# Retention and a gated feed-forward network on one core: k by tokens moves into a fifth slot beside v, loaded with it in one transfer, and the order of the work is planned anew

## The chip, the cores and the metric

The kernel runs on one core of one Trainium2 chip. The metric is the device time in microseconds (us), the median of several runs. TensorE is called PE in the profile, its weight loads PEld, VectorE DVE, ScalarE ACT, GpSimd POOL, and the queue that issues the transfers SP.

## The reference

The inputs are q, k, v of shape (4, 8, 768, 64), w_in (512, 1024), conv_w (3, 1024), w_out (1024, 512), all float32.

```python
for t in range(S):                       # retention, per batch and head
    state = gamma * state + k[t] (x) v[t]
    y[t] = scale * q[t] @ state
x = y, heads side by side                # (4, 768, 512)
h = relu(x @ w_in)                       # (4, 768, 1024)
conv_out[t] = sum over k of conv_w[k] * h[t + k - 1]
out = (h * sigmoid(conv_out)) @ w_out    # (4, 768, 512)
```

## The kernel before

**Attention.** The 3,072 tokens are cut into 24 chunks of 128, each into two halves of 64. For chunk n, `load_qk(n)` brings q and k with the head dimension on partitions (512 KB), and `load_kv(n)` brings k and v with tokens on partitions. Before the change these are two transfers of 256 KB with rows of 2 KB: k into a tile `kn` of its own, which has two buffers, and v into slot 2 of the chunk's tile `rw`, which has three. Slot 3 of `rw` takes the carried state. `scale_v` multiplies v by decay factors, `masked` masks the scores. `mix(n, s)` is one visit of PE to half s of chunk n: matmuls for the state (`ps_st`), for y (`ps_y`) and for the next chunk's scores (`ps_s`), 64 of 64x64 in a usual visit, each with a weight load. `carry` (ACT) copies the state for the next visit, `decay` (DVE) makes x, `x_head` (ACT) and `x_rest` (DVE or POOL) split it into two parts in tile `xu`.

**Feed-forward.** Two chunks make a unit u of 256 tokens, 12 in all. `mm1(u, f)` is 12 matmuls of 128x258 (L643) for one of 8 slices of the hidden width; `relu`, `conv_tap`, `conv_side`, `gate`, `gated`, `g_head`, `g_rest` follow on ACT and DVE. `mm2(u, t, p)` is 6 matmuls of 128x512 (L699) for output tile t and pair p of hidden slices. There are 96 of `mm1` and 96 of `mm2`. The weights arrive as 64-bit numbers in 16 slices of 512 KB (buffer `g`, shared with the gate's output) and are turned into two float32 parts by a chain on ACT and DVE. For the first `SUMMED` slices PE does the last sum (`w_sum`, L609 to L611).

**Order.** Nothing is scheduled at run time: each engine, and SP's queue, works through its list in order. A planner, `plan`, plays the program with given durations, buffer counts (`BUFS`), a load rate (`BYTE`), and limits and lead times (`ATT_RATE`, `CONV_RATE`, `WINDOW`, `SLACK` and others), and the tasks are written out in the order of the start times that it finds. Where it finds PE waiting early on, it puts in filler matmuls on a zero tile (`keep_warm`, L388, 128x512), which PE works through like any others. In `plan`, `load_kv(n)` takes a `kn` buffer that `mix(n-2, 1)` gives back, and `load_qk(n)` an `rw` buffer that `mix(n-3, 1)` gives back.

Of the kernel before, what the change touches and what calls it, by code (L numbers as in the profile page):

```python
# [16 lines left out]
B, H, S, D = 4, 8, 768, 64  # L17
DM, DFF = H * D, 1024
P = 128
C = 64  # L20
NC = S // P
NPAIR = H // 2
# [16 lines left out]

BUFS = {
    "rw": 3, "kn": 2, "x": 2, "xu": 3, "g": 6, "m": 3, "es": 1, "h": 30, "cv": 2, "ps_s": 1, "ps_y": 2, "ps_m": 2, "ps_o": 2,
}


PE, DVE, ACT, POOL, DMA = "PE", "DVE", "ACT", "Pool", "DMA"
BYTE = 1 / 360

LATENCY, SAME = {DMA: 2600, PE: 250}, {DMA: 0, PE: 50}  # L50
OTHER = 60
# [8 lines left out]
MIX = 950  # L60
USE = {"scores": 0.25, "mix": 0.5, "mm1": 0.98, "mm2": 0.98, "w_sum": 0.98}

ATT_FIRST, ATT_RATE = 25, 6.5

CONV_FIRST, CONV_RATE, CONV_LAG = 0, 12.5, 27
SUM_LEAD, SUM_LEAD_OUT = 70, 238
AHEAD = 5517
WINDOW = {PE: 21000, POOL: 44250, DMA: 47450}
STAY = 48
PACE = 1.6  # L70

SLACK = {
    "x_rest": 21500, "halo": 22000, "w_in": 54000, "w_out": 28000, "mix": 55000, "carry": 57000,
    "masked": 54000, "make_gy": -7000, "x_head": 39000, "scores": 57500, "g_rest": 52500, "scale_v": 19500,
    "conv_w": 59000,
}

VECTOR_V, VECTOR_X, SUMMED = 36, 10, 5


PORT = {"scale_v", "x_rest", "w_clamp", "w_shift", "w_sign", "w_power", "w_low", "w_rest", "w_add", "conv_side", "gated",
# [2 lines left out]
def has_state(n, s):  # L84
    return (n % NC, s) != (NC - 1, 1)


def list_tasks():
# [3 lines left out]
    def task(key, engine, ns, after=(), take=None, free=None):  # L92
        tasks[key] = (engine, ns, [a for a in after if a], take, free)

    for n in range(N_CHUNKS):
        b, c = divmod(n, NC)
        u = n // NT
        task(("load_qk", n), DMA, 4 * P * D * H * 2 * BYTE, [n and ("load_qk", n - 1)], take="rw")
        after = [n and ("load_kv", n - 1), ("load_qk", n)]
        task(("load_kv", n), DMA, 4 * P * D * H * 2 * BYTE, after, take="kn")  # L100
        vector = n < VECTOR_V
        task(("scale_v", n), DVE if vector else POOL, 690 if vector else 1230, [("load_kv", n)])
        if n == 0:
            for s in range(2):
                task(("scores", 0, s), PE, 485, [("load_qk", 0), s and ("scores", 0, 0)], take=None if s else "ps_s")
        task(("masked", n), DVE, 690, [("mix", n - 1, 1) if n else ("scores", 0, 1)], free="ps_s")
        for s in range(2):

            prev = (n, 0) if s else (n - 1, 1) if c else (n - 1, 0) if b else None
            after = [("scale_v", n), ("masked", n), prev and ("carry", *prev)]  # L110
            after += [("mix", n, 0) if s else n and ("mix", n - 1, 1)]
            after += [n + 1 < N_CHUNKS and ("load_qk", n + 1)]
            take = None if s else "ps_y" if n + 1 == N_CHUNKS else ("ps_y", "ps_s")
            free = ("rw", "kn") if s and c < NC - 1 else "rw" if s else "kn" if c == NC - 1 else None
            task(("mix", n, s), PE, MIX, after, take, free)
            if has_state(n, s):
                task(("carry", n, s), ACT, 370, [("mix", n, s)])
        if n == 0:
            task(("load_gy",), DMA, 4 * P * NPAIR * P * BYTE)
        elif n < NC:  # L120
            task(("make_gy", c), ACT, 1300, [("load_gy",)])
        task(("decay", n), DVE, 690, [("mix", n, 1), ("make_gy", c) if c else ("load_gy",)], "x", "ps_y")
        if n % NT == 0:
            task(("x_tiles", u), POOL, 60, [u and ("x_tiles", u - 1)], take="xu")
        task(("x_head", n), ACT, 620, [("decay", n), ("x_tiles", u)])
        vector = n < VECTOR_X
        task(("x_rest", n), DVE if vector else POOL, 690 if vector else 1280, [("x_head", n)], free="x")
        if n % NT == NT - 1 and u % NU + 1 < NU:
            task(("halo", n, 1), POOL, 620, [("x_rest", n), ("x_tiles", u + 1)])
        if n % NT == 0 and u % NU > 0:  # L130
            task(("halo", n, -1), POOL, 620, [("x_rest", n), ("x_tiles", u - 1)])
# [3 lines left out]
    for i in range(CONV + 1):  # L135
        big = i < CONV
        ns = lambda t: t if big else 90
        if big:
            task(("load_w", i), DMA, 8 * P * DM * BYTE, [i and ("load_w", i - 1)], take="g")
        else:  # L140
# [20 lines left out]
    for u in range(N_UNITS):  # L161
        x = [("x_tiles", u)] + [("x_rest", NT * u + t) for t in range(NT)]
        x += [u % NU and ("halo", NT * u - 1, 1), u % NU + 1 < NU and ("halo", NT * u + NT, -1)]
        for f in range(NF):
# [3 lines left out]
                take="ps_m", free="xu" if f == NF - 1 else None,  # L168
            )
            p, odd = divmod(f, 2)  # L170
# [3 lines left out]
                take=None if odd else "cv",  # L174
# [14 lines left out]
        for t in range(NT):  # L189
            halves = 2 if (u, t) == LAST else 1  # L190
            for h in range(halves):
                for p in range(NF // 2):
# [5 lines left out]
                        take=None if p else "ps_o", free="g" if t == NT - 1 and h == halves - 1 else None,  # L198
# [41 lines left out]
def plan(tasks):  # L240
# [15 lines left out]
    for i, k in enumerate(tensor_sequence(tasks)):  # L256
        place[k], late[k] = i, t
        t += tasks[k][1] * PACE
    for k in reversed(topo):
# [4 lines left out]
    free = dict(FIRST)  # L264
    slots = {name: [0.0] * n for name, n in BUFS.items()}
    ready = {engine: {} for engine in free}
# [8 lines left out]
    def earliest(k, engine, t):  # L275
        for name in several(tasks[k][3]):
            if not slots[name]:
                return None
            t = max(t, min(slots[name]))
        if k[0] in PORT:  # L280
            t = max(t, port)
        return max(t, free[engine] + (SWITCH if engine == PE and last != KIND[k[0]] else 0))
# [4 lines left out]
    while len(start) < len(tasks):  # L287
        best = None
        for engine, some in ready.items():
            found = []  # L290
            for k, t in some.items():
                if engine != PE or place[k] < head + AHEAD:
                    t = earliest(k, engine, t)
                    if t is not None:
                        rank = place[k] - STAY * (KIND[k[0]] == last) if engine == PE else late[k]
                        found.append((t, rank, k))
            if found:
                limit = min(found)[0] + WINDOW.get(engine, 0)
                t, _, k = min((x for x in found if x[0] <= limit), key=lambda x: x[1])
# [39 lines left out]
def retention_then_gated_ffn(  # L339
# [13 lines left out]
    nc = tc.nc  # L353
# [12 lines left out]
    gvf_sb = const.tile([P, NC, 3, NPAIR], F32, name="gvf_sb")  # L366
# [7 lines left out]
    def buf(name, shape, dtype=F32):  # L374
        return pool.tile(shape, dtype, name=name, bufs=BUFS[name])

    def ps_buf(name, shape=(P, 512)):
        return psum.tile(list(shape), F32, name=name, bufs=BUFS[name])

# [8 lines left out]
            nc.tensor.matmul(ps, warm, warm.unsqueeze(1).broadcast_to([P, 4, P]), start=True, stop=True)  # L388


    rw, kns, s_ps, st_ps, y_ps, xt, xs = {}, {}, {}, {}, {}, {}, {}

    flat = lambda a: a.rearrange("p a s g c -> p a (s g c)")

    @emits
    def load_qk(n):

        rw[n] = buf("rw", [P, 4, 2, NPAIR, C])
        if n == 0:
            nc.gpsimd.dma_start(gvf_sb, gvf)  # L400
            nc.gpsimd.dma_start(mask_sb, mask)
        nc.sync.dma_start(flat(rw[n][:, :2]), qk[n])

    @emits
    def load_kv(n):

        kns[n] = buf("kn", [P, 2, NPAIR, C])
        nc.sync.dma_start(kns[n].rearrange("p s g c -> p (s g c)"), kv[n][:, 0])
        nc.sync.dma_start(flat(rw[n][:, 2:3]), kv[n][:, 1:])

    @emits
    def load_gy():
# [8 lines left out]
    @emits  # L421
    def scale_v(n):
        (nc.vector if n < VECTOR_V else nc.gpsimd).tensor_tensor(  # L423
            out=rw[n][:, 2], in0=rw[n][:, 2], in1=gvf_sb[:, n % NC, :2].unsqueeze(3).broadcast_to([P, 2, NPAIR, C]),
            op=ALU.mult,
        )

# [10 lines left out]
    def of_state(n, s):  # L438
        b, c = divmod(n, NC)
        first = (c, s) == (0, 0)  # L440
        if first:
            st_ps[b] = psum.tile([P, NPAIR, D], F32, name="ps_st")
        for g, j in heads:
            r = HALF[j]
            yield st_ps[b][r, g], kns[n][r, s, g], rw[n][r, 2, s, g], first and g == 0, c == NC - 1

    def of_y(n, s):
        if s == 0:
            y_ps[n] = ps_buf("ps_y", (P, NPAIR, 2, C))

        alone = n % NC == 0 and s == 0
        for g in range(NPAIR):
            for part, (w, x) in enumerate([(2, 1)] if alone else [(2, 1), (3, 0)]):
                for j in range(2):
                    y, r = y_ps[n][HALF[1 - j], g, s], HALF[j]
                    yield y, rw[n][r, w, s, g], rw[n][r, x, s, g], part == 0, part == 1 or alone
# [27 lines left out]
    @emits  # L484
    def carry(n, s):

        nc.scalar.copy(rw[n + s][:, 3, 1 - s], st_ps[n // NC])  # L487

    @emits
    def decay(n):  # L490
# [213 lines left out]
    def put(u, t, h):  # L704
# [5 lines left out]
        nc.sync.dma_start(out[r0 : r0 + P, cs], o[:, :n])  # L710

    start, more = plan(list_tasks())
    keep_warm(WARM_UP)
    for k in sorted(start, key=start.get):
# [55 lines left out]
```

## Time and profile before

| what | value |
|---|---|
| runs | 373.07, 375.35, 375.55 us; median 375.35 us |
| the profiled execution | 375.01 us, span 373.2 us |
| granted clock | 1.00 |
| PE busy | 361.2 us, 97% of the span |
| DVE, ACT, POOL busy | 259.3, 201.2, 31.8 us |
| read from HBM, written | 33.98 MB, 6.29 MB |

The span runs from the first to the last instruction of the profiled execution; some 1.8 us of its time lie outside it. The page gives busy time by engine, the span in 40 slices of 9.3 us, the DMA queues, the chain that ended last, and groups of instructions with what ended the idle time before them. The trace can be asked for waits, for the chain in order of time, and for single stretches.

### The profile page before, as it was taken

To read this page: it belongs to the slowest core of one execution; us is meant where nothing else is said; L and a number is where in the kernel's file an instruction comes from. 1 tells how busy PE (TensorE), PEld (TensorE's weight loads), DVE (VectorE), ACT (ScalarE), POOL (GpSimd) and SP (SyncE) were. 2 spreads that over 40 slices of the span, in tenths; PEclk is the share of its full clock that TensorE was granted. 3 is DMA by queue.
4 is the path that set the end of the run, shared out by engine and by line. 5 is a ranking of instruction groups with operands and counts; after the bars stand their busy time and mean duration, and the time that the engine had idled before them with its cause. 6 is when DMAs were issued, how large, how long until landed. Compare 5 with 4: busy or idle time off the path is not lost.

```text
span 373.2 us, 10996 instructions
## 1 busy us (share of the span) xinstructions
PE 361.2 (97%) x4781; PEld 315.3 (84%) x4781; DVE 259.3 (69%) x479; ACT 201.2 (54%) x443; POOL 31.8 (9%) x60
## 2 busy tenths in 40 slices
PE   7989979999999999999999999999999999999996
PEld 5766649999999888888888889989998999888886
DVE  1567869879889999888665835855555565689730
ACT  1664454567547546656554535657455455566721
POOL 1010100000222103004001101203000000000000
PEclk9999999999999999999999999999999999999999
DMA  8878987501454334513431100101001010001111
GB/s 265 293 266 267 344 285 256 171 2 56 172 181 155 122 117 142 200 58 133 152 116 58 59 2 1 58 0 58 0 12 47 2 56 2 29 28 58 56 56 57
DMA packets 16817, 40.97 MB, mean 110 GB/s; under 512 B 2017, under 2 KB 2401, under 8 KB 16769
## 3 DMA queue, kind: packets, MB, share of 16 engines
q1 hardware_dynamic: 16704, 40.21, 30.5%
q8 instruction: 37, 0.61, 0.7%
q0 software_dynamic: 64, 0.07, 0.1%
q14 instruction: 12, 0.09, 0.1%
HBM read 33.98 MB, written 6.29 MB: 108 GB/s over the span
## 4 chain that ended last, share of the span: by engine, by line
PE 92%; DVE 2%; issue 2%; DMA 2%; ACT 1%; SPq 0%; ACTq 0%; DVEq 0%
PE ps_m L643 36%; PE ps_o L699 36%; PE ps_st L459 6%; PE ps_s L459 5%; PE ps_y L459 4%; PE ps_o L388 4%; DMA rw<-in_kv 2%; PE ps_m L609 1%; DVE cv L664 1%; ACT L670 0%; ACT cv L670 0%; PE ps_m L611 0%; PE ps_m L610 0%; DVE rw L479 0%; DVE g L685 0%
## 5 line engine op out<-in xcount | busy, mean ns | idle before, releaser
L699 PE MATMUL ps_o<-h,g 128*128 128x512 f32 (+1 forms) x600 | 145.3, 387 | 0.0
L643 PE MATMUL ps_m<-xu,wi_hi 128*128 128x258 f32 x768 | 144.1, 286 | 0.5 <-ACT h L652 0.5
L643 PEld LDWEIGHTS ps_m<-xu,wi_hi 128*128 128x128 f32 x768 | 122.3, 189 | 6.8 <-ACT h L652 0.7
L699 PEld LDWEIGHTS ps_o<-h,g 128*128 128x128 f32 x600 | 105.0, 188 | 19.9 <-ACT o_sb L708 0.4
L643 PE MATMUL ps_m<-xu,wi_lo 128*128 128x258 f32 x384 | 108.6, 283 | 0.9 <-issue 0.9
L664 DVE SCALAR_TENSOR_TENSOR cv<-h,cw_sb,cv 128x256 f32<-128x256 f32 x192 | 94.1, 518 | 16.5 <-ACT cv L659 14.6
L643 PEld LDWEIGHTS ps_m<-xu,wi_lo 128*128 128x128 f32 x384 | 72.7, 189 | 1.1 <-issue 1.1
L652 ACT ACTIVATE h<-ps_m 128x258 f32<-128x258 f32 x96 | 36.3, 379 | 43.7 <-PE ps_m L643 43.6
L459 PE MATMUL ps_y<-rw 64*64 64x64 f32 x1472 | 54.2, 221 | 3.3 <-issue 2.9
L659 ACT ACTIVATE cv<-h,cw_sb 128x256 f32<-128x256 f32 x96 | 46.9, 504 | 18.4 <-DVE g L685 18.3
L685 DVE TENSOR_TENSOR g<-cv,g 128x512 fp32r<-128x512 f32 x48 | 33.1, 689 | 28.6 <-ACT g L680 28.5
L459 PEld LDWEIGHTS ps_y<-rw 64*64 64x64 f32 x1472 | 47.1, 134 | 4.0 <-issue 3.5
L675 DVE TENSOR_TENSOR cv<-h,cv 128x512 f32<-128x512 f32 x48 | 33.1, 690 | 21.4 <-ACT cv L670 20.9
L680 ACT CAST g<-cv 128x512 fp32r<-128x512 f32 x48 | 29.7, 619 | 29.6 <-PE ps_o L699 24.1
L670 ACT ACTIVATE cv<-cv 128x512 f32<-128x512 f32 x48 | 30.2, 630 | 26.2 <-DVE cv L664 25.9
L459 PEld LDWEIGHTS ps_st<-rw,kn 64*64 64x64 f32 x704 | 24.2, 134 | 13.5 <-issue 4.3
L459 PE MATMUL ps_st<-rw,kn 64*64 64x64 f32 x704 | 30.6, 225 | 1.8 <-DVE rw L423 1.1
L459 PE MATMUL ps_s<-rw 64*64 64x64 f32 x768 | 31.0, 219 | 1.1 <-issue 1.1
L423 DVE TENSOR_TENSOR rw<-rw,gvf_sb 128x512 f32<-128x512 f32 x24 | 17.5, 730 | 18.4 <-DMA rw<-in_kv 18.2
L459 PEld LDWEIGHTS ps_s<-rw 64*64 64x64 f32 x768 | 26.6, 135 | 2.4 <-issue 2.3
L487 ACT COPY rw<-ps_st 128x256 f32<-128x256 f32 x44 | 16.2, 369 | 20.3 <-PE ps_st L459 17.4
L479 DVE TENSOR_TENSOR rw<-ps_s,mask_sb 128x512 f32<-128x512 f32 x24 | 16.5, 689 | 11.5 <-PE ps_y L459 10.7
(48 smaller groups left out, 225.2 us busy)
## 6 DMA issues: line engine op xcount, KB each, us to landing
rw<-in_qk SPq DMA_DIRECT2D x24, 512.0 KB, 4.8
kn<-in_kv SPq DMA_DIRECT2D x24, 256.0 KB, 3.3
rw<-in_kv SPq DMA_DIRECT2D x24, 256.0 KB, 4.0
out_y<-o_sb SPq DMA_DIRECT2D x23, 256.0 KB, 2.0
g<-in_w_in SPq DMA_DIRECT2D x8, 512.0 KB, 6.2
g<-in_w_out SPq DMA_DIRECT2D x8, 512.0 KB, 4.9
gy_sb<-in_gy SPq DMA_DIRECT2D x1, 256.0 KB, 8.4
out_y<-o_sb SPq DMA_DIRECT2D x2, 128.0 KB, 1.7
```

The source lines that it names most:

```text
L423: (nc.vector if n < VECTOR_V else nc.gpsimd).tensor_tensor(out=rw[n][:, 2], in0=rw[n][:, 2], in1=gvf_sb[:, n % NC, :2].unsqueeze(3).broadc ...
L459: nc.tensor.matmul(out, lhsT, rhs, start=start, stop=stop, skip_group_check=True)
L479: nc.vector.tensor_tensor(out=rw[n][:, 1], in0=s_ps.pop(n), in1=mask_sb.unsqueeze(1).unsqueeze(1).broadcast_to([P, 2, NPAIR, C]), op=ALU.mult,
L643: nc.tensor.matmul(h_ps[u, f][:, :UH], w[:, k, fs], x[:, k, :], start=(i == 0), stop=(i == len(products) - 1))
L652: nc.scalar.activation(hs[u, p][:, i], h_ps.pop((u, f))[:, :UH], AF.Relu)
L659: nc.scalar.activation(cvs[u, p][:, i], hs[u, p][:, i, 1 : U + 1], AF.Copy, scale=cw_sb[:, f, 1:2])
L664: nc.vector.scalar_tensor_tensor(out=cv, in0=h[:, k : k + U], scalar=cw_sb[:, f, k : k + 1], in1=cv, op0=ALU.mult, op1=ALU.add)
L670: nc.scalar.activation(cvs[u, p], cvs[u, p], AF.Sigmoid)
L675: nc.vector.tensor_tensor(out=cv, in0=hs.pop((u, p))[:, :, 1 : U + 1], in1=cv, op=ALU.mult)
L680: nc.scalar.copy(gs[u, p][:, 0], cvs[u, p])
L685: nc.vector.tensor_tensor(out=lo, in0=cvs.pop((u, p)), in1=hi.bitcast(F32), op=ALU.subtract)
L699: nc.tensor.matmul(ps, g[:, ts], w[f][:, cs], start=(f == 0 and i == 0), stop=(f == NF - 1 and i == 2))
```

## The change

k by tokens goes into slot 2 of `rw`, which gets a fifth slot; v moves to slot 3 and the carried state to slot 4. The tile `kn` is gone, and with it its buffers. `load_kv(n)` is one transfer of 512 KB in rows of 4 KB, and takes no buffer of its own: it only follows `load_qk(n)` by way of the tile that this one takes. The buffer counts of `x`, `g`, `m` and `cv` change, and the planner runs with 350 GB/s for 360 and with other limits, so that the whole order is new.

```diff
-BUFS = {
-    "rw": 3, "kn": 2, "x": 2, "xu": 3, "g": 6, "m": 3, "es": 1, "h": 30, "cv": 2, "ps_s": 1, ...
-}
+BUFS = {"rw": 3, "x": 6, "xu": 3, "g": 4, "m": 2, "es": 1, "h": 30, "cv": 3, "ps_s": 1, ...}
-BYTE = 1 / 360
+BYTE = 1 / 350
-ATT_FIRST, ATT_RATE = 25, 6.5
+ATT_FIRST, ATT_RATE = 28, 11.5
...
-VECTOR_V, VECTOR_X, SUMMED = 36, 10, 5
+VECTOR_V, VECTOR_X, SUMMED = 16, 38, 6
...
-        after = [n and ("load_kv", n - 1), ("load_qk", n)]
-        task(("load_kv", n), DMA, 4 * P * D * H * 2 * BYTE, after, take="kn")
+        task(("load_kv", n), DMA, 4 * P * D * H * 2 * BYTE, [n and ("load_kv", n - 1), ("load_qk", n)])
...
-            free = ("rw", "kn") if s and c < NC - 1 else "rw" if s else "kn" if c == NC - 1 else None
-            task(("mix", n, s), PE, MIX, after, take, free)
+            task(("mix", n, s), PE, MIX, after, take, "rw" if s else None)
...
-        rw[n] = buf("rw", [P, 4, 2, NPAIR, C])
+        rw[n] = buf("rw", [P, 5, 2, NPAIR, C])
...
-        kns[n] = buf("kn", [P, 2, NPAIR, C])
-        nc.sync.dma_start(kns[n].rearrange("p s g c -> p (s g c)"), kv[n][:, 0])
-        nc.sync.dma_start(flat(rw[n][:, 2:3]), kv[n][:, 1:])
+        nc.sync.dma_start(flat(rw[n][:, 2:4]), kv[n])
...
-            yield st_ps[b][r, g], kns[n][r, s, g], rw[n][r, 2, s, g], first and g == 0, c == NC - 1
+            yield st_ps[b][r, g], rw[n][r, 2, s, g], rw[n][r, 3, s, g], first and g == 0, c == NC - 1
...
-        nc.scalar.copy(rw[n + s][:, 3, 1 - s], st_ps[n // NC])
+        nc.scalar.copy(rw[n + s][:, 4, 1 - s], st_ps[n // NC])
```

With `VECTOR_X` 38 and `VECTOR_V` 16, every `x_rest` is on DVE (before, 14 of 24 were on POOL) and `scale_v` of chunks 16 to 23 is on POOL (before, none was).

SP's list at the start of the program, before, up to the fourth chunk's q and k:

```order
L402 DMA rw<-in_qk 128x1024
L408 DMA kn<-in_kv 128x512
L409 DMA rw<-in_kv 128x512
L402 DMA rw<-in_qk 128x1024
L408 DMA kn<-in_kv 128x512
L409 DMA rw<-in_kv 128x512
L402 DMA rw<-in_qk 128x1024
L413 DMA gy_sb<-in_gy 128x512
L532 DMA g<-in_w_in 128x1024
L408 DMA kn<-in_kv 128x512
L409 DMA rw<-in_kv 128x512
L402 DMA rw<-in_qk 128x1024
```

The third chunk's k and v stand behind the first slice of w_in. The same place of SP's list in the changed kernel:

```order
L399 DMA rw<-in_qk 128x1024 x2
L407 DMA gy_sb<-in_gy 128x512
L403 DMA rw<-in_kv 128x1024
L399 DMA rw<-in_qk 128x1024
L403 DMA rw<-in_kv 128x1024 x2
L526 DMA g<-in_w_in 128x1024
L399 DMA rw<-in_qk 128x1024
```

The first chunk's k and v now stand behind the second chunk's q and k and the table gy, and the third chunk's ahead of the weights.

PE's list at the start, before, from the first fillers to the first row of `mix(0, 0)`:

```order
L388 MATMUL ps_o<-o_sb 128x512 x9
L459 MATMUL ps_s<-rw 64x64 x16
L388 MATMUL ps_o<-o_sb 128x512 x7
L459 MATMUL ps_st<-rw,kn 64x64 x2
L459 MATMUL ps_y<-rw 64x64 x2
```

And in the changed kernel:

```order
L384 MATMUL ps_o<-o_sb 128x512 x9
L453 MATMUL ps_s<-rw 64x64 x16
L384 MATMUL ps_o<-o_sb 128x512 x14
L453 MATMUL ps_st<-rw 64x64 x2
L453 MATMUL ps_y<-rw 64x64 x2
```

Fourteen fillers stand ahead of the first visit in place of seven. After it, and up to `mm1(0, 3)`, there were 47 fillers in 12 groups, five `w_sum` and 17 visits; now there are 35 in 9 groups, six `w_sum` and again 17 visits, and the feed-forward work between the visits stands in eight places instead of five. From `mm1(0, 3)` on, both lists hold 93 of `mm1`, 96 of `mm2` and 31 visits, each visit by itself between feed-forward work; before, 20 visits are followed by an `mm1` and 11 by an `mm2`, and now 28 and 3, since the visits come earlier and the first `mm2` only after `mm1(4, 0)`.

SP's list where the last slices of w_out and the first outputs stand, in the changed kernel:

```order
L403 DMA rw<-in_kv 128x1024
L526 DMA g<-in_w_out 128x1024
L399 DMA rw<-in_qk 128x1024
L403 DMA rw<-in_kv 128x1024
L399 DMA rw<-in_qk 128x1024
L403 DMA rw<-in_kv 128x1024
L526 DMA g<-in_w_out 128x1024 x2
L399 DMA rw<-in_qk 128x1024
L403 DMA rw<-in_kv 128x1024
L704 DMA out_y<-o_sb 128x512 x23
```

The last two slices of w_out moved from between chunks 11 and 13 to just ahead of chunk 23, with all outputs behind them; the very last waits for the `g` buffer that `mm2(0, 1, 0)` gives back.

More of the change, by code (lines that the diff above doesn't have):

```diff
@@ L37 @@
 HALF = (slice(0, D), slice(D, P))
-BUFS = {
-    "rw": 3, "kn": 2, "x": 2, "xu": 3, "g": 6, "m": 3, "es": 1, "h": 30, "cv": 2, "ps_s": 1, "ps_y": 2, "ps_m": 2, "ps_o": 2,
-}
+BUFS = {"rw": 3, "x": 6, "xu": 3, "g": 4, "m": 2, "es": 1, "h": 30, "cv": 3, "ps_s": 1, "ps_y": 2, "ps_m": 2, "ps_o": 2}
 PE, DVE, ACT, POOL, DMA = "PE", "DVE", "ACT", "Pool", "DMA"
-BYTE = 1 / 360
+BYTE = 1 / 350
 LATENCY, SAME = {DMA: 2600, PE: 250}, {DMA: 0, PE: 50}
@@ L61 @@
 USE = {"scores": 0.25, "mix": 0.5, "mm1": 0.98, "mm2": 0.98, "w_sum": 0.98}
-ATT_FIRST, ATT_RATE = 25, 6.5
[L65 to L70, printed above, removed]
+ATT_FIRST, ATT_RATE = 28, 11.5
+CONV_FIRST, CONV_RATE, CONV_LAG = 27, 7.25, 24
+SUM_LEAD, SUM_LEAD_OUT = 47, 267
+AHEAD = 10094
+WINDOW = {PE: 73300, POOL: 92500, DMA: 89900, DVE: 200}
+STAY = 3
+PACE = 1.5
 SLACK = {
-    "x_rest": 21500, "halo": 22000, "w_in": 54000, "w_out": 28000, "mix": 55000, "carry": 57000,
-    "masked": 54000, "make_gy": -7000, "x_head": 39000, "scores": 57500, "g_rest": 52500, "scale_v": 19500,
-    "conv_w": 59000,
+    "x_rest": 60000, "halo": 21500, "w_in": 56500, "w_out": 2000, "mix": -7500, "carry": 10000,
+    "masked": -8000, "make_gy": 10500, "x_head": 23500, "scores": 10500, "g_rest": 2500, "scale_v": -8000,
+    "conv_w": 32000,
 }
-VECTOR_V, VECTOR_X, SUMMED = 36, 10, 5
+VECTOR_V, VECTOR_X, SUMMED = 16, 38, 6
 PORT = {"scale_v", "x_rest", "w_clamp", "w_shift", "w_sign", "w_power", "w_low", "w_rest", "w_add", "conv_side", "gated",
@@ L388, in keep_warm @@
             nc.tensor.matmul(ps, warm, warm.unsqueeze(1).broadcast_to([P, 4, P]), start=True, stop=True)
-    rw, kns, s_ps, st_ps, y_ps, xt, xs = {}, {}, {}, {}, {}, {}, {}
+    rw, s_ps, st_ps, y_ps, xt, xs = {}, {}, {}, {}, {}, {}
     flat = lambda a: a.rearrange("p a s g c -> p a (s g c)")
@@ L423, in scale_v @@
         (nc.vector if n < VECTOR_V else nc.gpsimd).tensor_tensor(
-            out=rw[n][:, 2], in0=rw[n][:, 2], in1=gvf_sb[:, n % NC, :2].unsqueeze(3).broadcast_to([P, 2, NPAIR, C]),
+            out=rw[n][:, 3], in0=rw[n][:, 3], in1=gvf_sb[:, n % NC, :2].unsqueeze(3).broadcast_to([P, 2, NPAIR, C]),
             op=ALU.mult,
@@ L452, in of_y @@
         for g in range(NPAIR):
-            for part, (w, x) in enumerate([(2, 1)] if alone else [(2, 1), (3, 0)]):
+            for part, (w, x) in enumerate([(3, 1)] if alone else [(3, 1), (4, 0)]):
                 for j in range(2):
```

## The prediction, made blind

> **What bounds the kernel now.** I first read the page's busy times and slices, then what PE waited for, then the chain in order of time, since only that tells a stage with slack from one without.
>
> ```profile
> PE 361.2 (97%) x4781; PEld 315.3 (84%) x4781; DVE 259.3 (69%) x479; ACT 201.2 (54%) x443; POOL 31.8 (9%) x60
> PEclk9999999999999999999999999999999999999999
> GB/s 265 293 266 267 344 285 256 171 2 56 172 181 155 122 117 142 200 58 133 152 116 58 59 2 1 58 0 58 0 12 47 2 56 2 29 28 58 56 56 57
> PE ps_st L459 <- DVE rw L423: 1.1, 1, 1.1
> SPq L408 <- PE ps_st L459: 95.0, 21, 8.9
> ```
>
> PE is busy for 97% at full clock. SP waited 95 us for `kn` buffers, but the only wait of PE that a load stands behind is one of 1.1 us, for the first scaled v. The load rate is high only until about 65 us. So the queue's 95 us are no time to be won: what counts is PE's own list, and whether something stops it.
>
> After 60 us the chain is PE matmul upon matmul. Pieces of it, with start and length:
>
> ```profile
> 96.89 2.87 PE ps_m L643 x24
> 105.02 1.63 PE ps_m L643 x12
> 107.74 1.63 PE ps_m L643 x12
> 121.73 1.41 PE ps_o L699 x6
> 369.92 0.37 ACT o_sb L708
> ```
>
> Two `mm1` in a row take 2.87, so 1.44 each. From one `mm1` to the next across a visit is 107.74 - 105.02 = 2.72, so a visit by itself costs 2.72 - 1.44 = 1.28: 1.09 of its own and 0.19 for the two switches. An `mm2` takes 1.41 after an `mm1`.
>
> **From `mm1(0, 3)` on: no change.** Both lists hold 93 `mm1`, 96 `mm2` and 31 lone visits there; the order among them is different, the sum is not (93 x 1.44 + 96 x 1.4 + 31 x 1.28 = 308 us, the last tile in halves in both). The one exception is a group of two fillers ahead of `mm1(0, 7)`, which goes: -0.7 by the rows below. In before this stage begins at 59.8 and ends with the copy at 369.92, so it runs within 2 us of that sum, and there is nothing in it to win. What is moved must stay hidden there, above all on DVE:
>
> ```profile
> L664 DVE SCALAR_TENSOR_TENSOR cv<-h,cw_sb,cv 128x256 f32<-128x256 f32 x192 | 94.1, 518 | 16.5 <-ACT cv L659 14.6
> L423 DVE TENSOR_TENSOR rw<-rw,gvf_sb 128x512 f32<-128x512 f32 x24 | 17.5, 730 | 18.4 <-DMA rw<-in_kv 18.2
> L512 DVE TENSOR_TENSOR xu<-x,xu 128x512 fp32r<-128x512 f32 x10 | 6.9, 688 | 1.9 <-ACT xu L506 1.9
> ```
>
> DVE gets 14 `x_rest` (0.69 each, +9.6), gives 8 `scale_v` to POOL (0.73 each, -5.8) and one slice's last two sums (-1.4): 2.4 us more of 259. The cover is the feed-forward's lag: the first `mm2` now stands after 33 `mm1`, so conv work may fall far behind without stopping PE. If DVE did set the pace in the alternation of visits and `mm1`, a pair of `mm1` and one chunk would cost it 4 x 0.69 + 4 x 0.52 + 2 x 0.69 = 6.2 us against PE's 2 x 2.72 = 5.4, so 0.8 us a chunk over ten chunks. I take nothing for it; 8 us is the upper end.
>
> **Up to `mm1(0, 3)`: fillers out, a later start.** The chain of before, and the two `scale_v` that show when v had landed:
>
> ```profile
> 8.18 0.69 DVE L423 TENSOR_TENSOR rw<-rw,gvf_sb 128x512 f32<-128x512 f32 x1 [7.18 <-DMA rw<-in_kv]
> 10.74 0.69 DVE L423 TENSOR_TENSOR rw<-rw,gvf_sb 128x512 f32<-128x512 f32 x1 [1.27 <-DMA rw<-in_kv]
> 8.27 0.52 issue
> 8.79 0.69 DVE rw L479
> 9.53 0.27 PE ps_y L459 x2
> 10.57 0.66 PE ps_o L388 x2
> 12.32 1.12 PE ps_o L388 x4
> 14.54 1.36 PE ps_o L388 x5
> 16.99 1.81 PE ps_o L388 x7
> 19.58 1.13 issue
> 30.30 0.83 issue
> 33.80 1.06 PE ps_m L609 x2
> 35.32 2.87 PE ps_m L643 x24
> 42.56 0.66 issue
> 48.86 0.86 issue
> 54.05 2.07 issue
> 59.86 2.24 PE ps_m L643 x17
> ```
>
> - *Start.* v of chunk 0 was there at 8.18, behind 1.05 MB, and that of chunk 1 at 10.74, behind 2.10 MB. Now chunk 0's k and v stand behind qk of two chunks and gy, 1.83 MB with themselves. Between the two rows that is 8.18 + 0.74 x 2.56 = 10.1: **+1.9**. Fourteen fillers end at about 6.0 + 0.2 + 14 x 0.23 = 9.4, so the load, not the fillers, ends this wait. Before, `masked(0)` came after `scale_v(0)` on DVE and held up y until 9.53; now it is ahead: -0.5. Bounds: +0.5 if the load comes with the fillers' end, +2.6 if as late as v of chunk 1.
> - *Fillers.* The four groups give 0.23 for one and 0.2 for a group. 12 fillers and 3 groups less: **-3.4**.
> - *Sixth `w_sum`.* From the first row of one (33.80) to the `mm1` behind it (35.32): **+1.5**.
> - *Three more places* of feed-forward work between visits, at 0.19: **+0.6**.
> - *Two fillers* ahead of `mm1(0, 7)`: **-0.7**.
>
> By PE's work the sum is 1.9 - 0.5 - 3.4 + 1.5 + 0.6 - 0.7 = **-0.6 us**.
>
> **The gaps called "issue".** Five of them after the first visit make 5.55 us. They lie within runs of matmuls, and nothing in the profile holds PE there. One row may tell what does:
>
> ```profile
> q8 instruction: 37, 0.61, 0.7%
> ```
>
> 37 packets for 9,562 matmuls and weight loads are 258 instructions each. A chunk has two visits of 128 instructions, so PE needs a packet per chunk, and these packets share the 16 engines with loads at 265 to 344 GB/s. No gap lies where the rate has fallen to 200 or less. I take the gaps as waits for instructions; that is an inference.
>
> The Trainium skill, in "Runtime: NRT & Kernel Launch", section "Instruction fetch mechanics", says that instructions come in blocks of 16 KiB or 256 instructions, and that crossing a block is mostly hidden. The size agrees with 0.61 MB in 37; "mostly hidden" does not, if the five gaps are this. By that rule alone the gaps are chance and the sum stays at -0.6.
>
> If so, the early stage is paced by packets, and filler time taken out comes back as gaps: the packets up to `mm1(0, 3)` are as many as before (24 filler instructions fewer of some 2,400). Then only the start and the late pair of fillers count: 1.9 - 0.7 = +1.2. Does the load behind a packet change? SP's rows say no:
>
> ```profile
> 11.89 0.33 SPq L408 DMA_DIRECT2D kn<-in_kv  x1
> 12.26 0.44 SPq L409 DMA_DIRECT2D rw<-in_kv  x1
> 12.87 0.33 SPq L402 DMA_DIRECT2D rw<-in_qk  x1
> ```
>
> Before, the end of one visit let go 1 MB at once: k and v of one chunk, and q and k of the next. Now it lets go q, k, and k, v of the same chunk, again 1 MB, once per chunk. So I keep 5.55 us of gaps, and take **+0.3**, the middle of -0.6 and +1.2.
>
> **The transfer itself.**
>
> ```profile
> rw<-in_qk SPq DMA_DIRECT2D x24, 512.0 KB, 4.8
> kn<-in_kv SPq DMA_DIRECT2D x24, 256.0 KB, 3.3
> rw<-in_kv SPq DMA_DIRECT2D x24, 256.0 KB, 4.0
> g<-in_w_out SPq DMA_DIRECT2D x8, 512.0 KB, 4.9
> gy_sb<-in_gy SPq DMA_DIRECT2D x1, 256.0 KB, 8.4
> ```
>
> One transfer of 512 KB in rows of 4 KB lands in 4.8 us from issue, by the first row; the two of 256 KB, 0.4 apart, are both there after about 4.4. The joined one is 0.4 later, or as early; but it is asked for a whole chunk sooner, so I take nothing. PE needs q and k of chunk n+3 at `mix(n+2, 0)`, and its own list between (four fillers, 1.09, two, 1.09, eight, at the tightest place) is 6.0 us against 4.8: cover of 1.2. A landing at 8.4, as gy had at its worst, would cost 2.4 once.
>
> **Sum.** The profiled execution took 375.01 us for a span of 373.2. 375.0 + 0.3 = **375.3 us**, which is also the median of the runs shown (375.35).
>
> **Rivals.**
>
> 1. *Loads set the early pace* (8%). With `kn` gone, SP no longer stops for it, and the stage could run at the best slice's 344 GB/s for the mean of 287 of the first six: 14 MB up to `mm1(0, 3)` in 41 us for 49, so 8 us less, 367. Against it: after 9.5 us no wait of PE names a load. The Trainium skill's "Perfetto Trace Analysis", section "DMA Optimizations", speaks for it, with batches of 4 KB for 2 KB as the first thing to do where a kernel is bound by DMA; its next item, that split transfers let some work start sooner, speaks against the change at the start, as the +1.9 does.
> 2. *The gaps close* (12%). Fewer transfers ahead of the packets or luck in their timing: -0.6 - 5.55, about 369. For it: the gaps are uneven, 0.66 to 2.07, so half of it (372) is as likely as all.
> 3. *Gaps spread into the alternation* (25%, the other side). After `mm1(0, 3)` come 19 visits alternating with `mm1`, 152 instructions per 2.72 us: a packet every 4.6 us, beside 1 MB of loads every 5.4 us (190 GB/s and more with weights). Before, this stretch had no gap:
>
> ```profile
> 100.00:120.00 20.00, 20.00 (x508) 18.71 (x497) 18.36 (x32) 10.87 (x27) 4.66 (x6) 1.00 0.47 164
> ```
>
>    It decides where a packet, behind the loads, takes longer than 4.6 us. Twelve packets at 1.1 each would be 13 us, every second one 6.6: 381 to 382. DVE's 8 us would end a little above.
> 4. *The last slice of w_out is late* (5%). It now waits for `mm2(0, 1, 0)` and must be loaded (4.9) and turned (some eight operations of at most 0.69 on ACT and DVE, so about 5, and an estimated 5 behind other work) before `mm2(0, 0, 3)`, 18 us of PE's list later. A delay of 6 us more would cost 3: 378.
>
> That SP's order does not do what it says is part of the forecast: loads do come a chunk sooner, to no use.
>
> **How the numbers follow.** The forecast has 50% and its own range is 372 to 379: gaps by 2.5 either way, the start's bounds, 1 us between runs. Rivals as given. A measurement can tell a change of about 1% here, 3.75 us: under 371.6 is faster, over 379.1 slower. Faster: rival 1, two thirds of rival 2 and a little of the forecast, 0.2. Slower: rival 3, some of 4, 0.27. The rest, 0.53. The range that leaves out 2 in 10 is 369.5 to 381.
>
> **What the profile after would show.** Right: first `ps_st` at 10.5 to 11.2; `mm1(0, 3)` at 59 to 61; 58 matmuls of L384; issue gaps of 4 to 7 us before that and none after; SP's waits down by most of the 95 us. Wrong: `mm1(0, 3)` before 57 (rivals 1 and 2), or PE idle between 60 and 110 us, by "issue" (rival 3) or by DVE.

## The result, and the profile after

| | before | after |
|---|---|---|
| median of 20 runs each, us | 375.35 | 378.78 |
| lowest and highest, us | 372.51, 377.4 | 376.34, 382.24 |
| the profiled execution: time, span, us | 375.01, 373.2 | 378.25, 376.5 |

The ratio of after to before is 1.0099, with a 95% interval of 1.0077 to 1.012. The kernel became about 1% slower; 375.3 was forecast. At equal granted clock the difference stays: the five runs of after at 1.00 have a median of 377.57, and the runs of before at 1.00, in the groups of the experiments below, medians of 372.9 to 373.9.

The page of after, first: busy times, clock and load rate by slice, and the queue that I took for the instructions.

```profile
PE 364.2 (97%) x4778; PEld 317.8 (84%) x4778; DVE 255.4 (68%) x483; ACT 202.1 (54%) x444; POOL 24.2 (6%) x54
PEclk9998999999999999999999999999999999999999
GB/s 301 276 246 231 259 307 201 290 192 223 129 269 177 198 190 144 29 57 3 3 56 2 29 30 0 57 0 56 1 28 31 0 57 0 30 28 56 57 56 56
q8 instruction: 37, 0.61, 0.6%
```

PE is again busy for 97%. Loads now keep a high rate up to about 150 us and not only to 65. The fourth slice has a lower clock. Next, what PE and SP waited for (engine, line and tile that waited, what it waited for: total, times, longest):

```profile
PE ps_y L453 <- issue: 2.7, 3, 1.5
PE ps_st L453 <- issue: 1.9, 2, 1.7
PE ps_s L453 <- issue: 1.3, 2, 0.9
PE ps_m L637 <- issue: 1.1, 1, 1.1
PE ps_y L453 <- DVE m L549: 1.0, 1, 1.0
SPq L399 <- PE ps_y L453: 97.9, 21, 6.9
```

No load is in PE's list. "issue" is, 7.0 us in all where before had 4.9; ahead of `mm1` it stands in both (0.9 before, at L643, and 1.1 after, at L637). SP waits as long as before: the `rw` buffer that a visit gives back has taken the place of `kn`.

Last, the chain in order of time: start, length, what. First the start and every piece called "issue" that is longer than 0.2 up to `mm1(0, 3)`, which begins at the last row here; then those from there to 130 us, and the end.

```profile
6.69 3.40 PE ps_o L384 x14
10.09 0.20 PE ps_st L453 x2
19.92 1.52 issue
30.37 1.73 issue
45.03 0.46 issue
51.55 0.43 DVE m L549
57.12 0.85 issue
61.03 1.51 PE ps_m L637 x11
```

```profile
89.64 1.07 issue
95.39 0.42 issue
109.80 0.69 issue
...
373.22 0.37 ACT o_sb L702
```

Ahead of the first visit stand the fourteen fillers, 3.40 us, and no load. Five gaps before `mm1(0, 3)` make 5.59 us (the one at 51 us, 1.03 of standstill from 51.03 on, is put down to a DVE operation on a tile that `ps_y` doesn't read). Three more, 2.18 us, lie behind it, among the visits that now alternate with `mm1`. Before there were none there.

A count settles what the gaps have in common. These are the numbers of the matmuls, counted from the program's start, at which a gap of over 0.25 us within a run of matmuls ended:

```
before  348   602   856   983  1109
after   349   604   856   983  1110  1871  1998  2379
```

Within 2, they lie at 94 + 127 k in both, though other work stands at these places in the two kernels. 127 matmuls with their weight loads are 254 instructions, about one of the 37 packets.

The kept traces also hold the times of each packet of queue q8 (all of 16,384 bytes). Beside the gaps, in us:

```
before  packet ended  19.45  29.65  41.81  48.45  54.72
        gap ended     20.71  31.13  43.22  49.72  56.12
after   packet ended  20.05  30.82  44.18  50.60  56.62  89.33  94.21  109.12
        gap ended     21.43  32.10  45.49  52.06  57.97  90.71  95.81  110.49
```

Every gap ends 1.3 to 1.6 us after a packet did, the one put down to DVE among them. These packets took 0.9 to 1.1 us each.

### The profile page after: what moved, and what is told of

The parts are those of the page before. It is cut to its first block, busy times and chain, and to the rows that moved or that the text cites. A ratio compares the mean times of both kernels' runs of the same rounds, so it can differ in the third digit from the quotient of the medians.

```text
span 376.5 us, 10959 instructions
## 1 busy us (share of the span) xinstructions
PE 364.2 (97%) x4778; PEld 317.8 (84%) x4778; DVE 255.4 (68%) x483; ACT 202.1 (54%) x444; POOL 24.2 (6%) x54
## 2 busy tenths in 40 slices
DMA packets 13359, 40.96 MB, mean 109 GB/s; under 512 B 1632, under 2 KB 2016, under 8 KB 13312
## 3 DMA queue, kind: packets, MB, share of 16 engines
q1 hardware_dynamic: 13248, 40.20, 29.6%
## 4 chain that ended last, share of the span: by engine, by line
PE 97%; issue 2%; ACT 0%; DVE 0%; ACTq 0%
PE ps_m L637 39%; PE ps_o L693 36%; PE ps_st L453 6%; PE ps_s L453 5%; PE ps_o L384 5%; PE ps_y L453 4%; PE ps_m L603 2%; PE ps_m L604 0%; PE ps_m L605 0%; ACT m L544 0%; ACT wi_lo L623 0%; DVE m L549 0%; ACT o_sb L702 0%; DVE o_sb L378 0%; ACTq L702 0%
## 5 line engine op out<-in xcount | busy, mean ns | idle before, releaser
L637 PE MATMUL ps_m<-xu,wi_hi 128*128 128x258 f32 x768 | 146.0, 287 | 1.1 <-issue 1.1
L637 PEld LDWEIGHTS ps_m<-xu,wi_hi 128*128 128x128 f32 x768 | 122.5, 189 | 7.3
L637 PE MATMUL ps_m<-xu,wi_lo 128*128 128x258 f32 x384 | 108.5, 283 | 0.0
L658 DVE SCALAR_TENSOR_TENSOR cv<-h,cw_sb,cv 128x256 f32<-128x256 f32 x192 | 85.5, 484 | 18.1 <-ACT cv L653 16.5
L637 PEld LDWEIGHTS ps_m<-xu,wi_lo 128*128 128x128 f32 x384 | 72.7, 189 | 1.2 <-issue 1.2
L453 PE MATMUL ps_y<-rw 64*64 64x64 f32 x1472 | 55.7, 223 | 3.7 <-issue 2.7
L453 PEld LDWEIGHTS ps_y<-rw 64*64 64x64 f32 x1472 | 48.1, 136 | 4.9 <-issue 3.6
L453 PEld LDWEIGHTS ps_st<-rw 64*64 64x64 f32 x704 | 25.0, 136 | 12.7 <-issue 7.2
L473 DVE TENSOR_TENSOR rw<-ps_s,mask_sb 128x512 f32<-128x512 f32 x24 | 16.6, 690 | 27.5 <-PE ps_y L453 12.8
L453 PE MATMUL ps_s<-rw 64*64 64x64 f32 x768 | 32.3, 221 | 1.3 <-issue 1.3
L453 PE MATMUL ps_st<-rw 64*64 64x64 f32 x704 | 31.7, 227 | 1.9 <-issue 1.9
L453 PEld LDWEIGHTS ps_s<-rw 64*64 64x64 f32 x768 | 27.5, 137 | 2.2 <-issue 1.6
L702 ACT COPY o_sb<-ps_o 128x512 f32<-128x512 f32 (+1 forms) x25 | 14.2, 567 | 12.9 <-PE ps_o L693 12.9
## 6 DMA issues: line engine op xcount, KB each, us to landing
rw<-in_qk SPq DMA_DIRECT2D x24, 512.0 KB, 3.7
rw<-in_kv SPq DMA_DIRECT2D x24, 512.0 KB, 5.1
g<-in_w_in SPq DMA_DIRECT2D x8, 512.0 KB, 6.7
g<-in_w_out SPq DMA_DIRECT2D x8, 512.0 KB, 5.9
```

Source lines behind the costliest of these rows:

```text
L453: nc.tensor.matmul(out, lhsT, rhs, start=start, stop=stop, skip_group_check=True)
L473: nc.vector.tensor_tensor(out=rw[n][:, 1], in0=s_ps.pop(n), in1=mask_sb.unsqueeze(1).unsqueeze(1).broadcast_to([P, 2, NPAIR, C]), op=ALU.mult,
L637: nc.tensor.matmul(h_ps[u, f][:, :UH], w[:, k, fs], x[:, k, :], start=(i == 0), stop=(i == len(products) - 1))
L658: nc.vector.scalar_tensor_tensor(out=cv, in0=h[:, k : k + U], scalar=cw_sb[:, f, k : k + 1], in1=cv, op0=ALU.mult, op1=ALU.add)
```

## The experiments

Each was timed in turn with runs of the kernel before, whose median was 374.59 to 375.62 in these groups; ratios are to that kernel.

### The layout alone, and the order alone

```diff
# before's parameters and list_tasks (with its kn) in the changed kernel
-BUFS = {"rw": 3, "x": 6, ...}; BYTE = 1 / 350; ATT_FIRST, ATT_RATE = 28, 11.5; ...
+BUFS = {"rw": 3, "kn": 2, "x": 2, ...}; BYTE = 1 / 360; ATT_FIRST, ATT_RATE = 25, 6.5; ...
```

> The order of before on every engine, with the new layout: k and v in one transfer into the five-slot tile. Theory (the loss comes from the new order: lower clock early, gaps among the visits that alternate with mm1): as before, 374 to 376 us, mm1(0, 3) at about 59.8 us, clock 1.00, five early gaps and none after 60 us. Rival (the joined transfer itself costs, by bigger bursts ahead of the instruction packets): 377 to 379 us.

Measured: 377.01, ratio 1.0049 [1.0014, 1.0083], at the rival's lower end: the joined transfer costs something without the new order.

```diff
# the changed kernel's order, with k by tokens in kn (three buffers) and two transfers
-        nc.sync.dma_start(flat(rw[n][:, 2:4]), kv[n])
+        kns[n] = buf("kn", [P, 2, NPAIR, C])
+        nc.sync.dma_start(kns[n].rearrange("p s g c -> p (s g c)"), kv[n][:, 0])
+        nc.sync.dma_start(flat(rw[n][:, 2:3]), kv[n][:, 1:])
```

> The new order, with the old layout: k in a tile of its own (three buffers, so that it never holds up a load that the new order asks for) and two transfers of 256 KB. Theory (order): as the change, 378 to 379.5 us, with the lower clock in some runs and gaps between 80 and 120 us. Rival (joined transfer): as before, 375 to 376 us.

Measured: 377.89, ratio 1.0076 [1.0037, 1.0114]. Each half of the change costs something by itself: the joined transfer about half a per cent, the order some three quarters, with intervals that overlap. What the joining adds in the new order (378.78 for 377.89) is within the noise. The new order keeps its gaps in the alternation with the old transfers, a little shorter. From its chain:

```profile
87.99 0.77 issue
93.85 0.36 issue
108.14 0.61 issue
```

### Light loads: are the gaps packets behind loads?

```diff
-        rw[n] = buf("rw", [P, 5, 2, NPAIR, C])
+        rw[n] = buf("rw", [P, 5, 2, NPAIR, C]) if n < 3 else rw[n - 3]
...
-        nc.sync.dma_start(flat(rw[n][:, :2]), qk[n])
+        w = slice(None) if n < 3 else slice(0, 64)
+        nc.sync.dma_start(flat(rw[n][:, :2])[:, :, w], qk[n][:, :, w])
# load_kv likewise
```

> The change, but from the fourth chunk on each load of q, k and v brings only an eighth of its columns (the rest of the tile keeps older data). Nothing on PE changes. Theory (PE's gaps are instruction packets held up behind loads): the gaps after 25 us go, some 4 us early and 2.3 us between 80 and 120 us, and with them the stretches of lower clock, 1.5 us: 370 to 372 us. Rival (the gaps belong to the instructions, loads or not): 378 us, gaps at the same places.

Measured: 365.97 (365.75 to 366.49), ratio 0.9741 [0.9711, 0.9772]: 12.8 us less than the changed kernel, where 7 to 9 were expected, and runs that hardly differ. (It leaves out most of q, k and v, so it is an experiment and not a version; so are the next two.) Its engines' shares of the chain, the start of `mm1(0, 3)`, and the stretch in which the new gaps lay (PE's busy time behind the length):

```profile
span 364.7 us, 10912 instructions
PE 99%; ACT 0%; issue 0%; DVE 0%; ACTq 0%
53.00 1.65 PE ps_m L639 x12
80.00:100.00 20.00, 20.00 (x569) 18.47 (x560) 17.16 (x31) 9.80 (x25) 5.23 (x7) 1.00 0.18 50
```

The same 20 us of after, where PE is 8 to 10 us further back in the same list, and loads run at 182 GB/s in place of 50:

```profile
80.00:100.00 20.00, 18.51 (x485) 16.98 (x474) 15.86 (x31) 10.66 (x24) 0.91 (x2) 1.00 0.51 182
```

There is no gap left. PE's list and the transfers' number are unchanged; only the bytes went, and the rows became shorter (and more: 18,735 packets in all for 13,359). So neither DVE nor PE's own work made the gaps.

As both lists are the same, the two traces can be matched matmul by matmul. After falls behind by 11.8 us in all. It begins its first visit 0.2 earlier. From there to `mm1(0, 3)` it loses 6.6 at the places 94 + 127 k, and 1.6 beside a fall of the clock (last section). Behind `mm1(0, 3)` it loses 3.7, all of it at five such places (k = 12, 14, 15, 18 and 25: 0.4, 1.2, 0.7, 1.0 and 0.3). The packets show why: the eight of after that have a gap behind them ended 3.4 to 5.3 us after PE had begun the block of instructions ahead of theirs, and the same eight with light loads 0.0 to 2.7 us after. They took 0.9 to 1.0 us each in both, so it is their start that comes late beside whole loads.

The same edit in the kernel before:

> The kernel before, but from chunk 3 on the loads of q, k and v bring only the first eighth of the columns (the rest of the tile keeps older data; its output is not the reference's). The same was done to the changed kernel, which then took 365.97. If the difference between the two kernels is instruction packets held up behind loads: no gaps within runs of matmuls, mm1(0, 3) at 52.6 (8.93 + 43.7 of work), and 366.7 to 368.2 in all, so that the changed order is now the faster one by 1 to 2 us, as its shorter list of fillers says. If the changed order is slower by its own work (switches, DVE, visits): the difference of 3.8 stays, and this run takes about 362.

Measured: 368.73 (368.37 to 368.9), ratio 0.9843 [0.9801, 0.9884], half a microsecond above the first of the two expectations and far from the second.

```profile
span 366.5 us, 10968 instructions
PE ps_y L461 <- issue: 0.9, 1, 0.9
53.20 1.88 PE ps_m L645 x14
```

One gap is left, at 13.5 us, behind the first three chunks, whose loads are whole. With light loads the changed kernel is the faster one, by 2.8 us. This refutes the other theory, that the new order is longer by its own work: it is shorter, and loses more than that to the packets and the clock.

Light loads from chunk 11 on only, in the changed kernel (`n < 11` for `n < 3`):

> The changed kernel with the loads cut to an eighth from chunk 11 on, so that only the loads after mm1(0, 3) are light (it leaves out most of the data of chunks 11 to 23). If the gaps at 89 to 110 us are packets behind loads: mm1(0, 3) at 61 as before, no gap after about 64, and 374.5 to 376 (378.8 less 2.3 of gaps and up to 3.7). If what was won by light loads in that stretch came from the early loads: 377.5 to 379.

Measured: 375.12, ratio 1.0002 [0.9967, 1.0037]: 3.7 us less than the changed kernel. Of its chain, one piece called "issue" is left behind `mm1(0, 3)`. It lies where q, k and v are light, but slices of w_out still come whole (144 GB/s in this slice of the page, 34 in the next):

```profile
67.70 0.45 issue
```

So the loads beside the alternation cost 3.7 us, and the earlier ones 9.1 (375.12 - 365.97), with what the clock lost.

### Fillers: is PE's work what paces the early stage?

```diff
+FILL = {("mix", 3, 1): 2, ("mix", 4, 0): 2, ("mix", 4, 1): 2, ("mix", 5, 0): 2, ("mix", 6, 0): 2, ("mix", 7, 1): 2}
...
+    for k in FILL:
+        more[k] = more.get(k, 0) + FILL[k]
```

> The change with 12 more filler matmuls between 28 and 58 us, in six groups, four of them new; by PE's work 12 x 0.23 + 4 x 0.2 = 3.6 us. Theory: the clock stays at 1.00 (-1.4 us), and part of the fillers lies where PE would wait for instructions anyway: 378 to 380 us. Rival (fillers only cost, the clock was no loss): 381.5 to 383 us. The early gaps stay at the same number of PE instructions from the start (matmul 603, 856, 982, 1109), and so lie at other work.

Measured: 378.9, ratio 1.0088 [1.0046, 1.013], the changed kernel's own time. Twelve more fillers in six places, four of which had none (12 x 0.23 + 4 x 0.2 = 3.6 us), cost nothing that the runs can tell (the interval reaches 1.6 us either way). From its chain, before `mm1(0, 3)`:

```profile
19.89 1.31 issue
30.97 1.12 issue
48.17 0.54 issue
```

The gaps are shorter by about 2.6 us: filler time and gaps stand for each other. The clock stayed at 1.00 in this trace, as the theory had it, which is worth another 1.6 against the trace of after.

### The first visit

```diff
     start, more = plan(list_tasks())
+    start[("load_kv", 0)] = start[("load_qk", 0)] + 0.001
```

> The changed kernel with the first chunk's k and v second in the queue, ahead of the second chunk's q and k and of gy. They should land at 5.8 to 6.5 in place of 7.9. mix(0, 0) then starts at 8.5 to 9.4 (the fourteen fillers end at about 9.4) in place of 10.0. If the early stage is paced by packets counted from the first visit: all of this is kept, 0.6 to 1.5 less, 377.3 to 378.2. If it is paced by the loads' bytes: the gaps grow by as much, 378.8.

Measured: 380.38, ratio 1.0139 [1.0083, 1.0195], not to be told from the changed kernel. A miss. The load landed 2.2 us sooner, at 5.7, but the fillers, `scale_v(0)` and the first `ps_st` stood like this (start and length):

```profile
7.09 3.48 PE L384 MATMUL ps_o<-o_sb 128*128 128x512 f32 x14
7.88 0.68 DVE L417 TENSOR_TENSOR rw<-rw,gvf_sb 128x512 f32<-128x512 f32 x1
10.51 0.27 PE L453 MATMUL ps_st<-rw 64*64 64x64 f32 x2
```

v was scaled at 8.56, and PE worked through fillers, which began 0.4 later than in after, for two more microseconds. It is the fillers that set the start, not the load.

### Smaller transfers

If packets wait behind loads, loads in smaller pieces may let them in sooner. In the kernel before, with 2 KB rows throughout:

```diff
-        nc.sync.dma_start(flat(rw[n][:, :2]), qk[n])
+        for a in range(2):
+            nc.sync.dma_start(flat(rw[n][:, a : a + 1]), qk[n][:, a : a + 1])
# each slice of the weights likewise, in two halves of its columns
```

> The kernel before with q and k loaded as two transfers of 2 KB rows, and each slice of the weights as two as well, so that all the large loads have rows of 2 KB. If a packet takes turns with the rows at its engine, it is let in sooner: gaps before mm1(0, 3) of 3 to 4.5 for 5.6, 373.5 to 374.8. If it waits for all that was queued before it: no change, 375.4. If the larger number of rows costs the loads time: gaps of 6 to 7, 376 to 377.

Measured: 372.52, ratio 0.9954 [0.9919, 0.9989]: faster than before. `mm1(0, 3)` begins 3.0 earlier, and PE's waits by "issue" ahead of attention's matmuls have come down to 2.0:

```profile
PE ps_y L460 <- issue: 2.0, 2, 1.4
```

The same in the changed kernel, k and v too:

> The changed kernel with every load of 512 KB (q and k, k and v, a slice of the weights) as two transfers with rows of 2 KB in place of one with rows of 4 KB. The same cut made the kernel before faster (372.5 for 375.5; gaps before mm1(0, 3) of 3.4 in place of 5.6). If packets take turns with rows at their DMA engine: gaps of some 4 to 5.5 in place of 7.8 over the whole kernel, 374.5 to 376. If the gain of the kernel before came from something that only its order has: 378 to 379.

Measured: 372.23, ratio 0.9931 [0.9895, 0.9968], 6.5 us less than the changed kernel and more than I had expected: the order itself is no loss once the packets get through.

With two transfers again, each taking every second kilobyte, so rows of 1 KB:

```diff
+            w = slice(256 * a, 256 * a + 256)
+            nc.sync.dma_start(flat(rw[n][:, :2])[:, :, w], qk[n][:, :, w])
```

> As the last one, with as many transfers, but each of them takes every second kilobyte, so that rows are of 1 KB. If packets take turns with rows: another step down, gaps of 2 to 3.5, 373 to 374.5. If it was the number of transfers that helped: as the last one, within 0.5. If short rows cost the loads time: loads take longer to land than the 3.7 to 6.7 of the changed kernel, PE waits for them, over 377.

Measured: 373.94, ratio 0.9988 [0.9961, 1.0015]. That lies in the range named for packets taking turns with rows, but it is no step down from 372.23. It does not decide: in its trace PE waited less by "issue" ahead of attention's matmuls than in that of the last run (3.2 us for 4.6), and more for ACT, DVE and POOL ahead of `ps_st` (4.0 for 1.2).

Two transfers of 64 partitions each, rows of 4 KB, in the kernel before:

```diff
-        nc.sync.dma_start(flat(rw[n][:, :2]), qk[n])
+        for r in HALF:
+            nc.sync.dma_start(flat(rw[n][:, :2])[r], qk[n][r])
# each slice of the weights likewise
```

> The kernel before with q and k, and each slice of the weights, in two transfers of 64 partitions each, rows of 4 KB as before: as many transfers as in the run with rows of 2 KB that took 372.5. If the size of the rows decides: no change, 375 to 376. If the number or the size of transfers decides: 372 to 373.

Measured: 389.36, ratio 1.0383 [1.0345, 1.0421], outside both expectations. It is no control, since such a transfer is slow by itself (KB each, median us to landing; the row for before is 512.0 KB, 6.2):

```profile
g<-in_w_in SPq DMA_DIRECT2D x16, 256.0 KB, 9.2
...
PE ps_y L460 <- issue: 7.8, 4, 3.7
```

The clock was at half for 10.2 us of this execution as well. The run shows only that slower loads come with longer gaps.

A cleaner pair in the changed kernel, with the weights left alone. First, q, k and k, v in two transfers of 256 KB each:

```diff
-        nc.sync.dma_start(flat(rw[n][:, 2:4]), kv[n])
+        for a in range(2):
+            nc.sync.dma_start(flat(rw[n][:, 2 + a : 3 + a]), kv[n][:, a : a + 1])
# q and k likewise
```

> The changed kernel with q and k, and k and v, in two transfers of 256 KB with rows of 2 KB each; the weights stay one transfer with rows of 4 KB. With the weights cut too it took 372.2. Two thirds of the large loads are cut, so two thirds of that gain: 374 to 375.5, by either theory (row size or number of transfers).

Measured: 374.04, ratio 0.9958 [0.9922, 0.9994]. Second, one transfer of 512 KB each, but into slots that are not adjacent:

```diff
-        nc.sync.dma_start(flat(rw[n][:, :2]), qk[n])
+        nc.sync.dma_start(flat(rw[n][:, 0:3:2]), qk[n])
...
-        nc.sync.dma_start(flat(rw[n][:, 2:4]), kv[n])
+        nc.sync.dma_start(flat(rw[n][:, 1:4:2]), kv[n])
# k and its masked scores now in slot 2, k by tokens in slot 1
```

> The changed kernel with one transfer of 512 KB each for q and k, and for k and v, as in the change, but into slots of the tile that are not adjacent (q 0, k by tokens 1, k 2, v 3), so that each row of 4 KB falls into two of 2 KB. If the size of the rows decides: as the run with two transfers, 374 to 375.5. If the number or size of the transfers decides: as the changed kernel, 378 to 379.5.

Measured: 379.05, ratio 1.0096 [1.0052, 1.0139]. The load queue's packets, its transfers of k and v, and a wait of PE, of the run with slots apart:

```profile
q1 hardware_dynamic: 19392, 40.20, 30.5%
rw<-in_kv SPq DMA_DIRECT2D x24, 512.0 KB, 5.7
PE ps_st L453 <- issue: 2.7, 2, 2.3
```

And of the run with two transfers:

```profile
q1 hardware_dynamic: 20160, 40.21, 31.2%
rw<-in_kv SPq DMA_DIRECT2D x48, 256.0 KB, 4.9
PE ps_st L455 <- issue: 1.7, 1, 1.7
```

The changed kernel has 13,248 packets there; both runs have the smaller rows (48 loads with 128 packets more each are the 19,392), and they differ by 5 us, 4.7 in the two traces. So it is the size or number of transfers that decides, not the rows.

The Trainium skill, in "Perfetto Trace Analysis", section "DMA Optimizations", puts larger pieces (2 KB to 4 or 8 KB) first and smaller ones, for an earlier start, second. Here the second held, with instruction packets as what got through sooner: joined, k and v cost half a per cent in the old order, and q and k as well as k and v cut apart won 4.7 us in the new one (378.78 to 374.04).

### A version that beats both

Transfers of 256 KB throughout, in the changed order, with an earlier first visit:

```diff
+    start[("load_gy",)] = start[("load_qk", 0)] + 0.001
+    start[("load_kv", 0)] = start[("load_qk", 0)] + 0.002
+    start[("make_gy", 4)] = start[("carry", 0, 0)] + 0.001
+    more[("mix", 0, 0)] = 8
```

> The changed kernel with rows of 2 KB, and with an earlier first visit: gy and then the first chunk's k and v second in the queue, 8 fillers for 14 ahead of mix(0, 0), and one table of gy made after the first carry instead of ahead of it. The fillers then end at 8.7 and v should be scaled by 8.2, so mix(0, 0) starts at 8.7 for 10.0. If the early stage is paced by packets counted from the first visit, or by PE's work: 1.3 less than the changed kernel with rows of 2 KB. If it is paced by the bytes of its loads: no gain, the gaps grow.

Measured: 371.73, ratio 0.9918 [0.9891, 0.9945]. It is 3.0 us under the kernel before in its group (374.76), and 7 under the changed kernel's median. Against the run without the earlier start (372.23) the half microsecond is within the noise: `mix(0, 0)` started at 9.52, since the mask landed only at 8.1. All that PE waited for by "issue":

```profile
PE ps_y L455 <- issue: 1.9, 2, 1.5
PE ps_s L455 <- issue: 0.7, 3, 0.3
```

## Why the prediction was wrong, point by point

The four traces, before and after, each whole and with light loads, split the difference. The start is that of the first `ps_y`, the middle that of `mm1(0, 3)`, the end the span. The first `ps_y` of after and of the two runs with light loads, before first:

```profile
10.03 0.27 PE L453 MATMUL ps_y<-rw 64*64 64x64 f32 x2
...
8.54 0.27 PE L461 MATMUL ps_y<-rw 64*64 64x64 f32 x2
...
10.27 0.27 PE L455 MATMUL ps_y<-rw 64*64 64x64 f32 x2
```

| us | before | after | before, light | after, light |
|---|---|---|---|---|
| to the first `ps_y` | 9.53 | 10.03 | 8.54 | 10.27 |
| from there to `mm1(0, 3)` | 50.33 | 51.00 | 44.66 | 42.73 |
| from there to the end | 313.3 | 315.5 | 313.3 | 311.7 |

| term, us | forecast | shown |
|---|---|---|
| start | +1.9 - 0.5 | +0.5 |
| PE's own work up to `mm1(0, 3)` | -1.3 | -1.0 |
| packets and clock, up to `mm1(0, 3)` | 5.55 kept, part of the gain lost | 6.6 before, 8.3 after: +1.7 |
| PE's own work behind it | -0.7 | -1.6 |
| packets behind it | 0 | 0 before, 3.8 after: +3.8 |

PE's own work is the stage's length with light loads, less the gap of 0.9 that before still has there; packets and clock are the rest of the stage with whole loads. The right-hand column adds up to +3.4; the spans differ by 3.3. Each trace is one execution, and runs of one kernel differ by more than some of these terms. By stage, the forecast of +0.3 is +1.0 up to `mm1(0, 3)` and -0.7 behind it; the traces show +1.2 and +2.2.

- **The step that failed is "From `mm1(0, 3)` on: no change".** PE's own work there did not grow, as it said (it fell by 1.6, of which 0.5 is a wait for ACT ahead of an `mm1` that only before has); but the sentence "there is nothing in it to win" passed over what there was to lose: the step put the wait for packets there at nothing. Dense visits bring a packet per 4.6 us and loads at the same time, and the packets came late. That is rival 3, with the place, the time and the cause as it put them. It was priced at 6.6 to 13 for every second or every packet; it cost 3.8, at five of the places 94 + 127 k; the three gaps of 1.07, 0.42 and 0.69 are 2.2 of it. At that price it would have given about 379, and the measured 378.8 lies there.
- **Gaps as waits for instructions: right,** and now shown, not inferred: the same matmul numbers in different orders, a packet's end 1.3 to 1.6 us ahead of each gap's, and no gap with light loads. The Trainium skill's "Runtime: NRT & Kernel Launch", section "Instruction fetch mechanics", has the right block (256 instructions; 254 from one gap's place to the next), but its "mostly hidden" fails here: the light loads took off 12.8 us, 3.4% of the time, with some 1.6 of clock in it by the two traces.
- **The early stage paced by packets: right in part, and its sum right by luck.** Fillers put in change the gaps and not the time. But the fillers taken out did not come back as gaps here: the gaps' sum was forecast at 5.55 and is 5.59 for 5.56, and PE's own work kept most of its gain (-1.0 of -1.3). What lengthened the stage is a term that no sum had, 1.6 of lower clock, below; it hides that the start came 0.9 under its forecast. The working has a slip too: "1.9 - 0.7 = +1.2" leaves out the start's -0.5, so that branch gives +0.7, and the middle of -0.6 and +0.7 is about zero.
- **The start: a smaller size, and another cause.** +1.4 was forecast for a late load; it came to +0.5 (the first `ps_st` at 10.09 on the chain, not 10.5 to 11.2), and to +1.7 with light loads, where before scaled its first v at 6.13 and not at 8.18. The load landed at 7.9, not at 10, and what PE waited for was its own fillers. That "the load, not the fillers, ends this wait" was wrong: fourteen of them took 3.40 where I had 3.2, and they began at 6.7, not 6.2.
- **The joined transfer at nothing ("so I take nothing"): wrong.** I priced its landing for PE's operands, and not what its size does to the packets: half a per cent in the old order.
- **SP's waits down by most of 95 us: wrong.** They stayed, at 97.9, on the `rw` ring. It cost nothing, as the part on the bound said of that number.
- **DVE and w_out: right that they stop nobody.** DVE was to get 2.4 us more and got 3.9 less (255.4 for 259.3), since its 192 `conv_tap` came down from 518 to 484 ns each; why is not shown. It has 15.86 and 14.12 of 20 us in the alternation, and the last slice of w_out stopped nobody.

## What to carry to other kernels

Where PE's instructions are small (64x64 here) and loads run at the same time, count instructions per microsecond as well as work. Gaps that came at equal numbers of instructions were packets held up beside loads. Filler work put into such a stretch cost nothing, and moving dense visits to where loads run made new gaps. Light loads, as an experiment, told at once how much was at stake; loads of 256 KB in place of 512 KB gave back about half of it.

## What the runs showed of the hardware that was not expected

- Two transfers of 256 KB in place of one of 512 KB, with the same rows of 2 KB, took 374.04 for 379.05. What in the transfer's size lets packets in is not shown.
- A slice of w_in cut into two transfers of 64 partitions landed after 9.2 us (the median of the halves), where one of 128 partitions took 6.2, and the kernel, with q and k cut in the same way, took 14.6 us more (389.36 to 374.76), part of it by a clock of 0.98 to 0.99.
- The clock can fall early on as well. In after the granted clock was at half for 3.4 us, from 33.30 on, behind the gap of 1.73 at 30.37; one of these microseconds, with the clock as the third figure from the end:

```profile
34.00:35.00 1.00, 1.00 (x3) 0.34 (x1) 0.00 (x0) 0.21 (x1) 0.00 (x0) 0.50 0.84 340
```

Matched with the run with light loads, the `w_sum` and the visits there took 1.6 us longer. The traces with light loads show no such fall, and their runs lie within 0.2% of each other, where those with whole loads spread over 1.3% and 1.6%. Yet such a gap does not always bring one: the run with light loads from chunk 11 on has the same gap of 1.73 at 30.73, and before has one of 2.07 at 54.05, and the clock stayed at 1.00 behind both. What brings it is not shown.
